# Light convolution and a routed mixture of experts in one kernel: fewer single blocks, more pairs, and later convolutions in the opening

## The chip, the cores and the metric

The kernel runs on one core of a Trainium2 chip. The metric is the device time of one execution in microseconds (us), as the median of the runs listed. The profiled execution is a run of its own; its page gives the span from its first to its last instruction.

An engine works through its own instructions in the order of the program: PE (matmul, with PEld for its weight loads), DVE (vector), ACT (activation), POOL (here the scatters) and SP (which issues the loads). One engine waits for another, or for a transfer, by semaphores.

## The reference

28,672 tokens (8 batches of 3,584) of 192 channels. First a causal convolution over 7 tokens, with the same normalised taps for the 24 channels of a head. Then each token goes to one of 8 experts, which is two dense layers of 192 to 1,024 to 192, with a gate.

```
w   = softmax over the taps of weight[h, :]                    # 8 heads, 7 taps
y   = sum over k of w[h, k] * x_padded[s + k]                  # lightweight convolution
logits = y @ w_gate ; local = sigmoid(y @ w_local)
e[s] = argmax(logits[s])  if s == 0 or local[s] < 0.5  else e[s-1]
out[s] = softmax(logits[s])[e] * (relu(y[s] @ w1[e]) @ w2[e])
```

All is float32. The expert of a token can be that of the token before it, so the choice is a scan over the sequence.

## The kernel before, in words

**Parts and units.** The tokens come in 16 parts of 1,792, numbered 0 to 15. For each part the kernel computes the convolution, the logits and the choice, and then a place for every token in a list in HBM named `slots`, in which each expert has its own region. A *unit* is 128 rows of one expert's region. Rows reach `slots` by scatters: `put()` issues one indirect DMA from POOL for 128 tokens (L844), 14 for a part, 16 for parts 0 and 1. The list `to_put` holds the scatters that have not been issued, in the order of the parts.

**Blocks.** The second half of the work is a list of *blocks* in program order, each 1, 2 or 4 units of one expert: a *single*, a *pair* or a *quad*. A block loads its expert's weights (1.5 MB, `wb`, `load_w`, L988) and its rows (`load_rows`), computes `hidden` (matmuls L1075) and `output` (L1097), scales by the gate, and scatters its rows to the result (`deliver`, L1125). The list is: 28 singles (parts 0 to 2), 43 pairs (the first of part 3), 19 quads of parts 9 to 14, then from the last part 4 quads, 4 pairs and 15 singles. Block numbers below count along this list from 0. `TURNED` is the number of opening singles, `FIRST` the number of singles and pairs before the quads. The quads go through `seven`, a scheme with seven products in place of eight (L1244), and `output_late` (L1294); the last pairs and singles through `hidden_late` (L1189) and `output_late`.

**Rows of singles and of pairs.** A single's rows come in one DMA (L996, 97.5 KB); PE transposes them (`turn`, L402) and ACT copies the result. A pair's rows come in four DMAs of 96 KB in pieces of 96 channels (L1004) and one for the heads (L1009); DVE transposes them (`turn_pair`, L1056). Both are loaded up to three blocks ahead (`ensure`, `AHEAD`). SP issues the row loads of a block, then the weights of the block three ahead. SP works in order, so a row load that waits for the part's scatters holds up what is behind it.

**When a part is ready.** `ensure(i)` looks at the blocks i to i + 3. If the part of block j is not routed, or has scatters left in `to_put`, it returns as long as j > i + 2; at j = i + 2 it finishes the route and issues the scatters that are left at once ("forced").

**The side work.** Convolution and choice of later parts run on DVE and ACT beside the blocks. They are Python generators that give a cost for each DVE instruction (0.68 for one of the convolution's, L440, of which a part has 36). At fixed places of each block `step(time)` takes instructions worth `time`: 2.1 and 1.3 in a single, 4.2, 1.2 and 3.4 in a pair. A route that is under way comes first, then the convolution. `start_conv` begins the next convolution when there is none; inside it, at the second of six channel groups (`b == 1`), the tokens of the next part are loaded (`load_x`, L150, 1.9 MB). The route begins with 96 small matmuls on PE (`logits`, L630) and ends with the places (`posi`, L810), after which the part's 14 scatters are in `to_put`, and with `tables`, which tell which expert each block has.

**Where the scatters are issued.** In a single: one in `hidden` and one in `output`. In a pair: three in `output`. The dictionary `spots` names the matmul behind which each is issued, and how many must be left over. The scatters of part 0 and the opening's route are written out by hand at the end (`puts_behind`: so many scatters behind an instruction of the route of part 1).

Of the kernel before, what the change touches and what calls it, by code (L numbers as in the profile page):

```python
# [24 lines left out]
NT = 14  # L25
PT = P * NT
NPART = N // PT
# [16 lines left out]
CAP = CAPU * UT  # L44
NU = (N + E * (UT - 1)) // UT
DUMMY = E * CAPU
EARLY = 3
SINGLES = 28
SPARE = 2


# [12 lines left out]
LAST = NPART - 1  # L64
PADS = NPART
NARROW = 8
PAIRED = 43
LEFT4 = E * (QT // 2 + UT // 8)
LEFTM = E * (QT // 2 + UT // 2)
LEFT2 = E * (BT // 2 + UT // 8)  # L70
# [41 lines left out]
def kernel(  # L112
# [35 lines left out]
    def load_x(g):  # L148
        x_sb = xs.tile([P, NX, D], F32, name="x_sb").rearrange("p t d -> p (t d)")
        nc.sync.dma_start(out=x_sb, in_=x[g])  # L150
        return x_sb.rearrange("p (b s) -> p b s", b=DQ)
# [75 lines left out]
    got, mark = {}, {}  # L227
# [125 lines left out]
    over = cst.tile([Q, Q], F32, name="over")  # L353
# [60 lines left out]
    def conv(g, x_sb):  # L414
        z = (z_tile() if g % 2 else
             ys[2].tile([P, NB, DG], F32, name="y_sb").rearrange("p b d -> p (b d)"))
        z = z[:, :NT * D].rearrange("p (b s) -> p b s", b=DQ)
        got[g] = z

        def chans(b, k):  # L420
            return x_sb[:, b, k * Q:(k + NT) * Q]

        at = {"b": 0, "first": 0}

        def firsts(more):
            while at["first"] <= min(at["b"] + more, DQ - 1):
                b = at["first"]
                nc.scalar.activation(z[:, b, :], chans(b, 0), Act.Copy, scale=c[:, b, 0:1])  # L428
                at["first"] += 1

        st["firsts"] = firsts
        firsts(0)
        yield 0
        for b in range(DQ):
            at["b"] = b
            firsts(0 if 0 < st["block"] < TURNED else 1)
            if b == 1 and 2 < g < NPART - 1:
                x_in[g + 1] = load_x(g + 1)
            for k in range(1, KC):
                nc.vector.scalar_tensor_tensor(z[:, b, :], chans(b, k), c[:, b, k:k + 1],  # L440
                                               z[:, b, :], Alu.mult, Alu.add)
                yield 0.68
# [175 lines left out]
    def logits(g, z):  # L618

        yield "pe"  # L620
        if late_p:
            both = st["bank"].tile([P, 2, 512], F32, name="ps")
            lps = [both[:, half, :TQ * Q] for half in range(2)]
        else:
            lps = [hps_p.tile([P, TQ * Q], F32, name="hps") for half in range(2)]
        begin = [min(TQ * j, NT - TQ) for j in range(4)]
        for b in range(DQ):
            for j in range(4):
                for half, rows in halves():
                    nc.tensor.matmul(lps[half][Q * j:Q * j + Q, :], lhsT=wgq[rows, b, :],  # L630
                                     rhs=z[rows, b, begin[j] * Q:(begin[j] + TQ) * Q],
                                     start=(b == 0), stop=(b == DQ - 1))
        ls = sm.tile([P, 2, TQ * Q], F32, name="ls", bufs=1)
        for half in range(2):
            nc.scalar.copy(ls[:, half, :], lps[half])
        y_sb = row_tile(g)[:, :NT, :]
        zt = z.rearrange("p b (t s) -> p t b s", s=Q)
        for t in range(0, NT, TQ):
            u = min(t + TQ, NT)
            nc.vector.transpose(y_sb[:, t:u, Y0:Y0 + D].rearrange("p t (b s) -> p t b s", s=Q),  # L640
                                zt[:, t:u])
            yield 0.24 * (u - t)
        st["turned"] = g
        lq = sm.tile([P, 2 * TQ, Q], F32, name="lq", bufs=1)
        nc.vector.transpose(lq.rearrange("p t e -> p (t e)"), ls.rearrange("p h x -> p (h x)"))
        yield 0.4
        lt = sm.tile([P, NT, E + 1], F32, name="lt")
        aside = g > EARLY + 2 and (st["cgen"] is not None or not late_p)
        if aside and late_p:
            yield "hop"  # L650
        for r in range(4):
            for j in range(4):
                t, u = TQ * j, min(TQ * (j + 1), NT)
                at = r // 2 * TQ + t - begin[j]
                e0 = r % 2 * (E + 1)
                dst = lt[Q * r:Q * r + Q, t:u, :]
                src = lq[Q * j:Q * j + Q, at:at + u - t, e0:e0 + E + 1]
                if aside:
                    nc.scalar.copy(dst, src)
                else:  # L660
                    nc.vector.tensor_copy(dst, src)
                    yield 0.12
            if aside:
                yield "hop"
        return y_sb, lt
# [166 lines left out]
    to_put = []  # L832
# [130 lines left out]
    FIRST = len(blocks)  # L963
# [2 lines left out]
    blocks += [(4, 2, i, LAST) for i in range(PAIRS)]  # L966
    blocks += [(5, 1, i, PADS) for i in range(REST)]

    AHEAD = 3
    TURNED = ONE[-1]  # L970
    SLOTS = 5
# [7 lines left out]
    def load_w(i):  # L979
# [5 lines left out]

        step = WA + WB if i > AHEAD else (WA + WB) // 3
        for x0 in range(0, WA + WB, step):
# [99 lines left out]
    def output(n, wb, xg, hT, w2):  # L1087

        yps = [yps_p.tile([P, 512], F32, name="yps") for half in range(2)]
        away = st["due"] and not (to_put and to_put[0][0] == EARLY)  # L1090
        spots = {1: {(0, 0, 1): 0} if st["block"] and not away else {},
                 2: {(0, 0, 0): 0, (0, 1, 1): 2, (2, 0, 7): 0}}[n]
        for m4 in ([0, 1, 4, 5], [2, 3, 6, 7]):
            for k in range(n):
                for m in m4:
                    for half, rows in halves():
                        ins = nc.tensor.matmul(yps[half][:, k * D:(k + 1) * D],  # L1097
                                               lhsT=hT[rows, m, k * P:(k + 1) * P],
                                               rhs=wb[rows, w2 + m * D:w2 + (m + 1) * D],
                                               start=(m == 0 and k == 0), stop=(m == FK - 1),  # L1100
                                               skip_group_check=True)
                    if len(to_put) > spots.get((m4[0], k, m), len(to_put)):
                        put(ins)
        o_sb = op.tile([P, KT, D], F32, name="o_sb")
        y = [[yps[half][:, k * D:(k + 1) * D] for half in range(2)] for k in range(n)]
        for k in range(n):
            nc.scalar.activation(o_sb[:, k, :], y[k][0], Act.Copy, scale=xg[:, k, 0:1])  # L1107

        step(1.2 if n > 1 or st["block"] > 1 else 0)
        for k in range(n):  # L1110
            nc.vector.scalar_tensor_tensor(o_sb[:, k, :], y[k][1], xg[:, k, 0:1], o_sb[:, k, :],  # L1111
                                           Alu.mult, Alu.add)

            st["hot"] = n == 1 and st["due"]
            if k == 0 and not st["hot"]:
                deliver(o_sb[:, 0, :], xg, 0)
            else:
                held.append(lambda ins, k=k: deliver(o_sb[:, k, :], xg, k, ins))
# [163 lines left out]
    def output_late(n, wb, xg, hT, rows_next=None, between=None):  # L1282

        for part, h in enumerate(hT):
# [34 lines left out]
    late_p = []  # L1319
    LATE = 3  # L1320
    SIDE = (2.4, 4.5, 2.0, 1.8)
    st = {"block": 0, "conv": 1, "cgen": None, "route": 1, "rgen": None, "routed": 1,
          "due": False, "hot": False, "since": 0, "bank": None, "over": 0, "turned": 1}

    def start_conv():
        g = st["conv"] + 1

        if (st["cgen"] is None and g < NPART and g <= st["turned"] + 2
                and (g != 3 or g in x_in and st["block"] > LATE + 2)):
            st["conv"] = g  # L1330
            st["cgen"] = conv(g, x_in.pop(g))
            next(st["cgen"])
# [48 lines left out]
    hot = hotp.tile([P, 2, NB, UT], F32, name="hot")  # L1381
# [23 lines left out]
    def puts_behind(ins, n):  # L1405
        for _ in range(n):
            put(ins)
# [7 lines left out]
    def ensure(i):  # L1415

        for j in range(len(xgs) + i, min(i + AHEAD + 1, len(blocks))):
            if j >= FIRST and j > i + 2:
                return
            g = blocks[j][3]  # L1420
            while st["routed"] < g or any(p[0] <= g for p in to_put):
                if j > (i + 2 if j < FIRST else i + 1):
                    return
                if st["routed"] < g:
                    step(4.2, late_p[0] if late_p else None, force=True)
                put()
            xgs[j] = load_rows(j)
# [10 lines left out]
    loaded = [0]  # L1438
    weights(AHEAD - 1)

# [1 line left out]
    picks = [yps_p.tile([P, 512], F32, name="yps")]  # L1442
    gather(0, ya, picks[0], range(4))
    rest(wide1)
    puts_behind(mark["lt", 1], 3)
    route1 = wide_route(1, yb, got.pop(1))
    some(route1, 2)
    taps_begun()
# [5 lines left out]
    picks.append(yps_p.tile([P, 512], F32, name="yps"))  # L1454
    gather(1, ya, picks[1], range(9))
    next(route1)
    puts_behind(mark["nf", 1], 2)
    step(1.8)
    xT, _ = turn(blocks[0][1], xgs[0])
    gather(1, ya, picks[1], range(9, NB))  # L1460
# [2 lines left out]
    step(2.4)  # L1463
    xgs[1] = gathered(picks[1])
    next(route1)
    puts_behind(mark["upto", 1], 4)
    next(route1)
    for i, (_, n, _, _) in enumerate(blocks):
        st["block"] = i
# [184 lines left out]
```

## Time and profile before

| | |
|---|---|
| time, median of 3 runs | 1298.71 us (1297.5 to 1300.3) |
| the profiled execution: time, span | 1300.09 us, 1298.3 us |
| granted TensorE clock | 0.999 |
| PE busy, PE weight loads busy | 1263.3 us (97%), 1206.5 us (93%) |
| DVE, ACT, POOL busy | 952.3 us (73%), 545.5 us (42%), 558.1 us (43%) |
| DMA | 299.59 MB, 231 GB/s over the span |
| weight loads | 109 of 1,536 KB and 12 of 512 KB |

The page names for each group of instructions the line of the kernel, the engine, the tiles, the count, busy time and idle time ahead of it, and who ended that idle time. A query of the trace gives the busy time of each engine in a stretch that one names, or the instructions of an engine in the order of time. A matmul's own duration overlaps its neighbours', so the length of a block is read from the start of its first matmul to the start of the next block's.

### The profile page before, as it was taken

The numbers are of one execution on the slowest core, as the hardware profiler recorded it, in microseconds if no ns is written. First come the engines' busy times: TensorE is split into PE (matmuls) and PEld (weight loads), VectorE is DVE, ScalarE is ACT, GpSimd is POOL, SyncE is SP. The second block draws the span as 40 slices with busy tenths as digits, with TensorE's granted clock in tenths as the row PEclk, the third lists the DMA queues.
The fourth block names the chain that finished last, engine by engine and source line by source line (L and its number), as shares of the span: only waits on it lengthen the run. The fifth ranks groups of instructions, "written<-read, shape, count | busy, mean of one in ns | idle before, by whom it ended". The sixth has DMA issues, their size and how long they took to land. (4 is left out here: it accounts for less than half of the span.)

```text
span 1298.3 us, 39551 instructions
## 1 busy us (share of the span) xinstructions
PE 1263.3 (97%) x15406; PEld 1206.5 (93%) x15406; DVE 952.3 (73%) x2504; ACT 545.5 (42%) x1208; POOL 558.1 (43%) x619
## 2 busy tenths in 40 slices
PE   9899989999999999999999999999999999999997
PEld 7789988998999999999999998999999999999997
DVE  5979878999898989999897999985885444431111
ACT  5345554334243442434425444543444444432332
POOL 4544354444344444444445455345466533421211
PEclk9999999999999999999999999999999999999999
DMA  5799997999787887978888546464655635536894
GB/s 196 262 364 390 340 359 238 341 322 321 225 288 266 248 289 228 292 260 252 288 228 243 157 122 178 105 180 123 167 158 156 183 103 158 155 97 194 276 323 156
DMA packets 182674, 299.59 MB, mean 231 GB/s; under 512 B 145872, under 2 KB 157191, under 8 KB 166738
## 3 DMA queue, kind: packets, MB, share of 16 engines
q1 hardware_dynamic: 160160, 251.79, 61.4%
q0 software_dynamic: 22320, 45.22, 10.7%
q8 instruction: 123, 2.02, 0.7%
q14 instruction: 69, 0.57, 0.1%
q10 hardware_dynamic: 2, 0.00, 0.0%
HBM read 251.35 MB, written 46.07 MB: 229 GB/s over the span
## 5 line engine op out<-in xcount | busy, mean ns | idle before, releaser
L1125 POOL DMA_INDIRECT out_dram<-o_sb,head x201 | 209.0, 1040 | 445.7 <-DVE o_sb L1309 269.1
L1075 PE MATMUL hps<-xT,wb 64*128 64x256 f32 (+1 forms) x3408 | 317.7, 337 | 4.7 <-issue 3.2
L1097 PE MATMUL yps<-wb,hT 64*128 64x192 f32 x3648 | 316.1, 324 | 3.7 <-DVE o_sb L1111 2.7
L1097 PEld LDWEIGHTS yps<-wb,hT 64*128 64x128 f32 x3648 | 301.6, 187 | 8.9 <-DVE o_sb L1111 3.9
L1075 PEld LDWEIGHTS hps<-xT,wb 64*128 64x128 f32 x3408 | 281.1, 187 | 30.7 <-issue 8.0
L1294 PE MATMUL ps<-wb,hot 64*128 64x192 f32 x3680 | 308.0, 323 | 0.9 <-issue 0.4
L844 POOL DMA_INDIRECT slots<-y_sb,posi x228 | 232.6, 1020 | 170.3 <-PE yps L1097 75.8
L1294 PEld LDWEIGHTS ps<-wb,hot 64*128 64x128 f32 x3680 | 299.3, 187 | 4.9 <-issue 2.5
L1084 ACT ACTIVATE hT<-hps 128x512 f32<-128x512 f32 (+1 forms) x284 | 130.4, 510 | 160.1 <-PE hps L1075 128.3
L440 DVE SCALAR_TENSOR_TENSOR y_sb<-x_sb,c,y_sb 128x448 f32<-128x448 f32 x252 | 172.7, 695 | 21.9 <-ACT y_sb L428 15.8
L440 DVE SCALAR_TENSOR_TENSOR z<-x_sb,c,z 128x448 f32<-128x448 f32 x252 | 172.8, 695 | 20.8 <-ACT z L428 11.6
L1309 DVE SCALAR_TENSOR_TENSOR o_sb<-ps,head,o_sb 128x192 f32<-128x192 f32 x115 | 43.2, 411 | 136.5 <-ACT o_sb L1304 130.3
L1304 ACT ACTIVATE o_sb<-ps,head 128x192 f32<-128x192 f32 x115 | 43.0, 418 | 204.2 <-PE ps L1294 198.3
L1107 ACT ACTIVATE o_sb<-yps,head 128x192 f32<-128x192 f32 x86 | 31.5, 417 | 155.6 <-PE yps L1097 79.8
L1168 DVE STREAM_TRANSPOSE xT<-y_sb 128x768 f32<-128x768 f32 (+1 forms) x65 | 54.8, 871 | 54.6 <-PE ps L1189 33.0
L1244 PE MATMUL ps<-xT,wb 64*128 64x256 f32 x736 | 88.6, 376 | 1.1 <-DVE xT L1220 1.1
L1244 PEld LDWEIGHTS ps<-xT,wb 64*128 64x128 f32 x736 | 77.7, 187 | 2.1 <-issue 1.5
L1189 PE MATMUL ps<-xT,wb 64*128 64x128 f32 (+1 forms) x912 | 64.3, 294 | 0.1
L1265 DVE TENSOR_TENSOR hot<-xps,hot 128x512 f32<-128x512 f32 x46 | 31.5, 685 | 44.7 <-PE xps L1244 44.6
L1125 POOL DMA_INDIRECT out_dram<-o_sb,xg x28 | 30.1, 1076 | 78.0 <-DVE o_sb L1111 52.0
L1189 PEld LDWEIGHTS ps<-xT,wb 64*128 64x128 f32 x912 | 62.7, 188 | 0.4 <-DVE xT L1168 0.4
L1266 ACT ACTIVATE hot<-hot 128x512 f32<-128x512 f32 x46 | 29.0, 630 | 64.9 <-DVE hot L1265 55.7
(296 smaller groups left out, 1399.8 us busy)
## 6 DMA issues: line engine op xcount, KB each, us to landing
wb<-in_w_dram SPq DMA_DIRECT2D x109, 1536.0 KB
x_sb<-in_x_dram SPq DMA_DIRECT2D x14, 1920.0 KB
y_sb<-slots SPq DMA_DIRECT2D x92, 192.0 KB
hot<-slots SPq DMA_DIRECT2D x172, 96.0 KB
wb<-in_w_dram SPq DMA_DIRECT2D x12, 512.0 KB
slots<-y_sb,posi POOLq DMA_INDIRECT x228
out_dram<-o_sb,head POOLq DMA_INDIRECT x201
x_sb<-in_xb_dram SPq DMA_DIRECT2D x4, 768.0 KB
```

The lines of the kernel that those rows point to most:

```text
L440: nc.vector.scalar_tensor_tensor(z[:, b, :], chans(b, k), c[:, b, k:k + 1], z[:, b, :], Alu.mult, Alu.add)
L844: ins = nc.gpsimd.indirect_dma_start(out=slots[:, :], in_=rows, in_offset=None, out_offset=bass.IndirectOffsetOnAxis(ap=to, axis=0)).ins
L1075: ins = nc.tensor.matmul(hps[half][:, j, w], lhsT=wb[rows, w1 + f0:w1 + f0 + P], rhs=xT[rows, d, w], start=(d == 0 and j == 0), stop=(d == ...
L1084: nc.scalar.activation(hT[:, m:m + 2, w], hps[half][:, :, w], Act.Relu)
L1097: ins = nc.tensor.matmul(yps[half][:, k * D:(k + 1) * D], lhsT=hT[rows, m, k * P:(k + 1) * P], rhs=wb[rows, w2 + m * D:w2 + (m + 1) * D], ...
L1125: sent = nc.gpsimd.indirect_dma_start(out=out, in_=o, in_offset=None, out_offset=bass.IndirectOffsetOnAxis(ap=xg.bitcast(I32)[:, k, 1:2], ...
L1168: nc.vector.transpose(xT.rearrange("p d (j t) -> p j d t", t=Q)[:, js], rows[:, js].rearrange("p j (d t) -> p j d t", t=Q))
L1189: nc.tensor.matmul(hps[:, half, j, :], lhsT=wb[rows, f0:f0 + P], rhs=xT[rows, d, :], start=(d == 0 and j == 0), stop=(d == KD - 1), skip_g ...
L1244: ins = nc.tensor.matmul(to[:, half, j, :], lhsT=b[rows, j * P:(j + 1) * P], rhs=a[rows, :], start=(first and j == 0), stop=True, skip_gro ...
L1294: ins = nc.tensor.matmul(yps[:, half, k * D:(k + 1) * D], lhsT=h[two][rows, side, j, k * P:(k + 1) * P], rhs=wb[rows, f * D:(f + 1) * D], ...
L1304: nc.scalar.activation(o_sb[:, k, :], yps[:, 0, k * D:(k + 1) * D], Act.Copy, scale=xg[:, at + k, 0:1])
L1309: nc.vector.scalar_tensor_tensor(o_sb[:, k, :], yps[:, 1, k * D:(k + 1) * D], xg[:, at + k, 0:1], o_sb[:, k, :], Alu.mult, Alu.add)
```

## The change

Three things change in the plan and four in the order of the work.

- `EARLY` 3 to 2, `SINGLES` 28 to 21, `PAIRED` 43 to 46. By the plan's arithmetic the list becomes 21 singles (parts 0 and 1), 46 pairs (3 of part 2, then 7 a part for parts 3 to 8, one of part 9), the same 19 quads, 4 quads, 5 pairs and 14 singles. The number of units computed stays 229; the blocks are 109 in place of 113.
- In the convolutions of parts 3 and 4 the tokens of the next part are loaded at `b == 3` in place of `b == 1`.
- A convolution of part 4 or later begins only when the block number is more than two past the block in which its tokens were loaded; this ends with the quads.
- The scatters of part 3 ("the fourth part") get more places: two more in `output` of a single or a pair, which makes three in a single and five in a pair.
- `ensure` finishes a part two blocks ahead only if no more than 3 of its scatters are left; else one block ahead. For single blocks nothing changes.
- In the opening, of the scatters of part 0 one more is issued behind `lt` and one more behind `nf`, and two fewer behind `upto`.
- `ASIDE = 5` keeps the old value of `EARLY + 2`, and the test against `EARLY` in `output` becomes a test against 3, as it was.

```diff
-EARLY = 3
-SINGLES = 28
+EARLY = 2
+SINGLES = 21
...
-PAIRED = 43
+PAIRED = 46
...
-            if b == 1 and 2 < g < NPART - 1:
+            if b == {3: 3, 4: 3}.get(g, 1) and 2 < g < NPART - 1:
                 x_in[g + 1] = load_x(g + 1)
+                st["loaded"] = st["block"]
...
-        aside = g > EARLY + 2 and (st["cgen"] is not None or not late_p)
+        aside = g > ASIDE and (st["cgen"] is not None or not late_p)
...
-        away = st["due"] and not (to_put and to_put[0][0] == EARLY)
+        away = st["due"] and not (to_put and to_put[0][0] == 3)
         spots = {1: {(0, 0, 1): 0} if st["block"] and not away else {},
                  2: {(0, 0, 0): 0, (0, 1, 1): 2, (2, 0, 7): 0}}[n]
+        if to_put and to_put[0][0] == 3:
+            spots.update({1: {(2, 0, 3): 0}, 2: {(2, 0, 2): 0, (2, 1, 6): 0}}[n])
...
         if (st["cgen"] is None and g < NPART and g <= st["turned"] + 2
+                and (late_p or g < 4 or st["block"] > st["loaded"] + 2)
                 and (g != 3 or g in x_in and st["block"] > LATE + 2)):
...
             while st["routed"] < g or any(p[0] <= g for p in to_put):
-                if j > (i + 2 if j < FIRST else i + 1):
+                wait = sum(p[0] <= g for p in to_put) if st["routed"] >= g else NT
+                if j > (i + 2 if j < TURNED or j < FIRST and wait <= 3 else i + 1):
                     return
...
-    puts_behind(mark["lt", 1], 3)
+    puts_behind(mark["lt", 1], 4)
...
-    puts_behind(mark["nf", 1], 2)
+    puts_behind(mark["nf", 1], 3)
...
-    puts_behind(mark["upto", 1], 4)
+    puts_behind(mark["upto", 1], 2)
```

3 lines of the change are left out of this document (2 added, 1 removed).

## The prediction

> **What bounds the kernel now.** I read the page first (busy shares and slices), then the busy time by stretches, then PE, SP, POOL and DVE in the order of time around the blocks that change. PE is busy almost everywhere, so a change is worth what it does to the length of the blocks on PE, and what makes PE wait.
>
> ```profile
> span 1298.3 us, 39551 instructions
> ...
> PE 1263.3 (97%) x15406; PEld 1206.5 (93%) x15406; DVE 952.3 (73%) x2504; ACT 545.5 (42%) x1208; POOL 558.1 (43%) x619
> ...
> DVE  5979878999898989999897999985885444431111
> ...
> DMA  5799997999787887978888546464655635536894
> ```
>
> The reader sees that from slice 2 to slice 20 (65 to 680 us) DVE runs near 90% too, and DMA at 70% and more: the opening singles and the pairs. Next the stretches, cut at the first matmul of a block. Columns: length, busy time of PE, PEld, DVE, ACT, POOL with instruction counts, clock, DMA share, GB/s.
>
> ```profile
> 162.16:167.60 5.44, 5.44 (x87) 5.44 (x86) 4.94 (x19) 2.89 (x9) 3.09 (x3) 1.00 0.85 286
> 173.04:182.09 9.05, 6.16 (x89) 5.78 (x87) 8.22 (x13) 3.70 (x11) 4.50 (x5) 1.00 0.84 293
> 182.09:227.35 45.26, 42.75 (x683) 40.23 (x680) 35.11 (x123) 21.07 (x66) 21.09 (x21) 1.00 0.79 288
> 260.63:271.01 10.38, 10.38 (x116) 9.85 (x115) 9.60 (x44) 3.09 (x7) 3.05 (x4) 1.00 1.00 307
> 227.35:305.52 78.17, 77.39 (x977) 71.92 (x977) 74.24 (x182) 26.93 (x56) 32.72 (x33) 1.00 1.00 327
> ...
> 695.53:863.40 167.87, 163.65 (x1828) 156.89 (x1826) 151.54 (x338) 80.79 (x137) 80.80 (x84) 1.00 0.54 145
> 1008.66:1168.23 159.57, 159.57 (x1732) 157.55 (x1731) 68.46 (x114) 68.65 (x96) 58.89 (x65) 1.00 0.51 140
> 1178.61:1188.99 10.38, 10.38 (x116) 10.38 (x115) 1.72 (x3) 2.90 (x6) 1.95 (x2) 1.00 0.59 191
> 1215.45:1220.73 5.28, 5.28 (x84) 5.28 (x83) 0.99 (x2) 1.74 (x5) 0.97 (x1) 1.00 0.78 234
> ```
>
> In this order: single 18 undisturbed, block 20 (the last single before part 2), the seven singles of part 2 (21 to 27), a pair undisturbed, the first seven pairs, the first eight quads, eight quads without side work, a pair and a single of the end. A pair costs PE 10.38 where two opening singles cost at least 10.88; and the seven singles took 45.26 where seven undisturbed ones take 38.08.
>
> **1. Seven singles become three pairs.** The seven singles hold one route's 96 small matmuls, and so will the three pairs (part 4's). What these cost between two pairs is seen here:
>
> ```profile
> 227.35 5.45 PE L1075 MATMUL hps<-xT,wb 64*128 64x256 f32 x48 [0.52 <-issue]
> 232.64 5.37 PE L1097 MATMUL yps<-wb,hT 64*128 64x192 f32 x64
> 237.84 5.35 PE L1075 MATMUL hps<-xT,wb 64*128 64x256 f32 x48
> 243.02 5.37 PE L1097 MATMUL yps<-wb,hT 64*128 64x192 f32 x64
> 248.32 1.90 PE L630 MATMUL hps<-z,wg 64*32 64x128 f32 x96
> 250.14 1.14 PE L1075 MATMUL hps<-xT,wb 64*128 64x256 f32 x8
> ```
>
> Block 29 goes from 237.84 to 250.14, 12.30, so the route adds 1.92. Three pairs: 3 x 10.38 + 1.92 = 33.06, against 45.26: **-12.2**. Do pairs stall as these singles did (5.3 beyond 38.08 + 1.92)? The first seven pairs took 78.17; less 72.66 for seven undisturbed, that is 5.51 for two routes, 2.76 each, and nothing else. So the bound on the dear side is 0.8 more, -11.4. DVE's transposition of a pair's rows (0.98, row below) replaces PE's; in 78.17 us DVE was busy 74.24 with it, so it is covered. Each pair also loads weights once for two units; four weight loads go in all.
>
> **2. One unit more at the end.** 229 units stay. The front's singles and pairs take 21 + 92 = 113 in place of 28 + 86 = 114, so the end has 14 singles and 5 pairs for 15 and 4: 10.38 - 5.28 = **+5.1**. Nothing waits there: PE is busy for all of both rows.
>
> **3. The wait in block 20.** Block 20 took 9.05 where 5.44 is undisturbed, 3.61 lost. PE, then POOL, then SP:
>
> ```profile
> 167.60 2.88 PE L1075 MATMUL hps<-xT,wb 64*128 64x128 f32 x48
> ...
> 173.04 3.50 PE L1075 MATMUL hps<-xT,wb 64*128 64x128 f32 x48
> 179.29 0.34 PE L402 MATMUL xps<-ident,xg 64*128 64x64 f32 x4 [2.74 <-DMA xg<-slots]
> ...
> 166.20 1.15 POOL L844 DMA_INDIRECT slots<-y_sb,posi  x1 [0.71 <-PE yps L1097]
> ...
> 163.75 0.33 SPq L988 DMA_DIRECT2D wb<-in_w_dram  x1
> 164.14 1.30 SPq L150 DMA_DIRECT2D x_sb<-in_x_dram  x1
> 175.01 1.25 SPq L996 DMA_DIRECT2D xg<-slots  x2
> ```
>
> Part 2's last scatter ended on POOL at 167.35, but SP could issue the rows only at 175.01, 7.66 later: weights and part 5's tokens had gone out just ahead. The change moves these tokens twelve convolution instructions on, into block 20 and on SP behind the rows and weights of block 23. How a pair's rows then come is bounded by part 3's in the run before, where only weights (issued at 210.99) were ahead:
>
> ```profile
> 214.97 0.96 POOL L844 DMA_INDIRECT slots<-y_sb,posi  x1 [0.30 <-issue]
> ...
> 210.99 0.33 SPq L988 DMA_DIRECT2D wb<-in_w_dram  x1
> 220.38 2.37 SPq L1004 DMA_DIRECT2D hot<-slots  x4
> 222.80 0.40 SPq L1009 DMA_DIRECT2D head<-slots  x1
> ...
> 226.32 0.98 DVE L1056 STREAM_TRANSPOSE xT<-hot 128x768 f32<-128x768 f32 x1 [1.31 <-DMA hot<-slots]
> ```
>
> Scatter's end to first row load 4.45, from there to the transposition 5.94, itself 0.98. For block 21: 167.35 + 4.45 + 5.94 + 0.98 = 178.7, and block 20 undisturbed ends at 178.5. So 0.2 is lost in place of 3.61: **-3.4**. The other bound: the 7.66 stays, then 181.9 against 182.09, -0.2. I take the first, as the weights alone were ahead in its row too.
>
> **4. Part 3 at block 24.** It is wanted sooner: 182.09 - 3.4 + 33.06 = 211.8, where block 28 had it at 227.35. Its places are there in good time:
>
> ```profile
> 160.89 0.17 DVE L810 CAST posi<-pos 128x14 int32<-128x14 f32 x1
> ...
> 172.07 0.99 POOL L844 DMA_INDIRECT slots<-y_sb,posi  x1 [0.30 <-issue]
> ```
>
> Its first scatter went at 172.07, behind part 2's, its last (above) ended at 215.93. With the new places blocks 19 and 20 issue three each, block 21 five, and the last three are forced when block 22 begins, at about 189.1. A scatter takes 0.96 and 0.30 to the next; with a delivery among them the last ends by 194.5. With the slow 7.66: 194.5 + 7.66 + 5.94 + 0.98 = 209.1, 2.7 before it is wanted; with 4.45, 5.9. So nothing is lost; without that cover each us late is a us of PE. On POOL five scatters and two deliveries are 7 x 1.3 = 9.1 of a pair's 10.38; the deliveries behind them wait, and two result buffers of two units each give them a block's time. On SP the row loads of 24 and 25 hold up the weights of block 25, wanted only at 222. Cost 0.
>
> **5. Later loads, the three blocks.** A convolution is 36 x 0.68 = 24.5 of step time, of which a single gives 3.4 and a pair 8.8. That of part 4 begins one block later (block 14) and by these costs still ends in block 21; that of part 5 begins in block 23, and the steps of 21 and 22 go partly unused. DVE gains nothing from having more to do there, and part 4 is wanted at block 31 only. What is late next is the quads. Each hold pushes the later parts back, and by the step costs part 13's logits come in the second quad, where they came just before the last pair:
>
> ```profile
> L630 PE MATMUL hps<-z,wg x576: 266/269/295, 136.4 to 684.8; 64*32 64x128 f32 x192
> ```
>
> (684.8 is the last in the opening's PSUM tiles.) Counted in steps, 13 quads in place of 11 have full side work. The first eight quads took 167.87 - 159.57 = 8.3 longer than eight without side work, less 1.92 for a route 6.4, 0.8 a quad: **+1.6**. Bounds: 0, and 4 if five quads stall.
>
> **6. The opening's scatters.**
>
> ```profile
> 51.68 0.94 POOL L844 DMA_INDIRECT slots<-y_sb,posi  x1 [0.30 <-issue]
> 52.92 0.94 POOL L844 DMA_INDIRECT slots<-y_sb,posi  x1 [0.30 <-issue]
> ```
>
> Two of the last four move ahead, so the last ends two issues of 1.24 sooner, 2.5. The rows that wait for them are block 2's, and PE has two blocks without them; I take 0, with -2.5 as the bound.
>
> **Sum.** -12.2 + 5.1 - 3.4 + 1.6 = -8.9. The profiled execution: span 1298.3 to 1289.4 (its time, 1300.09, is 1.8 above its span). Against the median of the runs shown, 1298.71, which is 1.4 under the profiled run: 1289.8.
>
> **Rivals.**
>
> *The wait in block 20 stays.* For it: the pair's rows take five DMAs in place of one, and the weights of 163.75 are still ahead of the scatter. Against it: 4.45 in the row above. It takes back 3.2: 1293.0. [...]
>
> *The first pairs are bound by DMA.* For it: the DMA share of a pair is 1.00, that of single 18 0.85, and blocks 21 to 24 have part 5's tokens and the faster scatters on top. While only rows were read, DMA moved little:
>
> ```profile
> 220.40:224.30 3.90, 3.90 (x65) 3.90 (x63) 2.92 (x12) 1.09 (x4) 1.41 (x3) 1.00 0.66 155
> ```
>
> 155 GB/s against 307. Against it: at a share of 1.00 the first seven pairs lost nothing that isn't their routes'. If blocks 21 to 27 each lost 1 us: 1296.8. [...]
>
> *Part 3 misses block 24* (the other side). If more than 3 scatters are left when block 22 begins, `ensure` returns and they are forced at block 23 (199.5). With 8 left the last ends at about 209.7; + 7.66 + 5.94 + 0.98 = 224.3, 12.5 late: 1302.3. It decides from a last scatter that ends after 206, where the loss passes 8.9. Against it: by the counts only three are left.
>
> *More is gained*: the 2.5 of the opening reaches PE, and the quads cost nothing more: 1285.7.
>
> **How the numbers follow.** Forecast 0.55, by itself 1287.5 to 1292; the wait stays 0.19; DMA-bound 0.07; part 3 misses 0.06; more gained 0.13. 0.2% is 2.6 us, about what a measurement of this kernel can tell from no change. Under 1296.1 lie the forecast, the wait, the greater gain and a small part of the DMA case: 0.88; within, most of the DMA case: 0.06; slower, part 3: 0.06. Low 1285.7, down to the greater gain; high 1295.5, past the wait and short of the two dear cases.
>
> **What would show it.** Block 21 starts by 178.5 to 179 and its rows load at about 172 (3); the pairs from 21 are 10.4 each, with one route 12.3 (1); block 24 starts at about 212 and its DVE transposition waits for no DMA (4); three sets of logits lie in the quads, and the first quad begins 15.6 sooner than 695.53 (5); 5 pairs and 14 singles at the end (2). Wrong would be a wait of PE at block 21 or 24 for `hot`, row loads of block 24 after 205, or pairs of 11 and more between 178 and 290.

## The result, and the profile after

The changed kernel took 1309.52 us (median of 19 runs, 1304.99 to 1314.6), the kernel before 1300.53 us beside it (19 runs, 1296.27 to 1306.67). The ratio is 1.0067, with a 95% interval of 1.0051 to 1.0083: slower by 0.7%, where 0.7% faster had been forecast. The profiled execution took 1311.33 us, with a span of 1309.6 us and a granted clock of 0.991 (0.999 before). The page's rows that answer to those of before:

```profile
span 1309.6 us, 39043 instructions
...
PE 1268.4 (97%) x15186; PEld 1209.1 (92%) x15186; DVE 955.6 (73%) x2507; ACT 535.6 (41%) x1164; POOL 557.4 (43%) x619
...
DVE  5879886998989989999898988984887435421111
...
DMA  5799988968787888978897636455564645546794
```

PE has 220 matmuls less than before and is busy 5 us longer, where the clock is lower: the 115 or 116 matmuls of a pair are busy 10.38 at a clock of 1.00 (block 21) and 13.02 at 0.88 (block 30). Where, the stretches tell. Busy time by stretches of the changed kernel (length, busy time of PE, PEld, DVE, ACT, POOL with counts, clock, DMA share, GB/s), cut as before: block 20, blocks 21 and 22, the three new pairs together, blocks 30 and 36, the 43 pairs from block 24, all quads.

```profile
175.56:184.23 8.67, 7.01 (x85) 5.89 (x83) 5.98 (x10) 2.62 (x7) 5.96 (x7) 1.00 0.78 180
184.23:194.61 10.38, 10.38 (x115) 9.85 (x115) 10.06 (x16) 2.60 (x5) 5.12 (x5) 1.00 1.02 386
194.61:214.25 19.64, 16.48 (x210) 14.06 (x210) 7.94 (x24) 3.89 (x9) 6.76 (x7) 0.83 0.73 250
184.23:224.63 40.40, 37.24 (x434) 33.67 (x434) 26.94 (x77) 10.12 (x22) 13.99 (x14) 0.92 0.86 303
289.34:304.09 14.75, 13.02 (x116) 11.65 (x114) 13.47 (x42) 4.01 (x8) 6.89 (x7) 0.88 0.94 307
357.99:372.50 14.51, 12.90 (x115) 11.55 (x114) 11.82 (x39) 2.90 (x6) 8.10 (x8) 0.88 0.58 185
224.63:696.27 471.64, 467.29 (x5587) 438.20 (x5587) 430.02 (x1186) 183.17 (x446) 209.79 (x205) 0.99 0.83 263
696.27:1174.46 478.19, 468.72 (x5260) 453.35 (x5259) 329.49 (x739) 212.65 (x329) 225.25 (x241) 1.00 0.54 150
```

Block 21 is the 10.38 of the forecast. Block 22, a pair with one route (12.3 forecast), took 19.64 at a clock of 0.83; blocks 30 and 36, plain pairs, 14.75 and 14.5 at 0.88. These three are 16 us longer than such blocks undisturbed, where forecast and result lie 20 us apart. The instructions of block 22 in order of time, PE, then ACT, then POOL:

```profile
194.61 5.35 PE L1077 MATMUL hps<-xT,wb 64*128 64x256 f32 x48
202.84 3.56 PE L631 MATMUL hps<-y_sb,wg 64*32 64x128 f32 x70 [2.89 <-ACT hT L1086]
...
202.19 1.08 ACT L1086 ACTIVATE hT<-hps 128x512 f32<-128x512 f32 x2 [5.96 <-remote]
...
194.88 0.96 POOL L845 DMA_INDIRECT slots<-y_sb,posi  x1 [0.74 <-PE yps L1101]
196.14 0.96 POOL L845 DMA_INDIRECT slots<-y_sb,posi  x1 [0.30 <-issue]
197.41 0.98 POOL L1129 DMA_INDIRECT out_dram<-o_sb,head  x1 [0.30 <-issue]
198.69 0.96 POOL L845 DMA_INDIRECT slots<-y_sb,posi  x1 [0.30 <-issue]
199.96 0.96 POOL L845 DMA_INDIRECT slots<-y_sb,posi  x1 [0.30 <-issue]
201.23 0.96 POOL L845 DMA_INDIRECT slots<-y_sb,posi  x1 [0.30 <-issue]
```

The first half of `hidden`'s 48 matmuls had ended by 197.4, but the trace records the semaphore updates that they raise only at 202.11 and 202.15, almost five microseconds late, and ACT read the result from 202.19. In those microseconds POOL issued six indirect transfers back to back, 0.30 apart, and the last ended at 202.19. Block 30, PE and POOL:

```profile
294.52 2.27 PE L1101 MATMUL yps<-wb,hT 64*128 64x192 f32 x25
297.73 0.32 PE L1101 MATMUL yps<-wb,hT 64*128 64x192 f32 x1 [0.93 <-issue]
298.45 0.32 PE L1101 MATMUL yps<-wb,hT 64*128 64x192 f32 x1 [0.40 <-issue]
299.17 5.09 PE L1101 MATMUL yps<-wb,hT 64*128 64x192 f32 x37 [0.40 <-issue]
...
291.96 0.96 POOL L845 DMA_INDIRECT slots<-y_sb,posi  x1 [7.40 <-issue]
...
297.07 0.98 POOL L1129 DMA_INDIRECT out_dram<-o_sb,head  x1 [0.30 <-issue]
```

Five transfers from 291.96 to 298.05, again without a pause; PE waits for nothing that the profile shows ("issue"), goes on at 299.17 and then has the half clock (0.50) from 299.6 to 303.0. Block 36 is the same with five from 360.33 to 366.41. In its first trace the kernel before has no run of five after its opening.

**Two kinds of chip.** The later runs, each set on one chip beside the kernel before, met a difference without which no number below can be read. The last column counts, in the profiled trace of the kernel named, the matmuls that raise a semaphore and have no recorded update of it within 1 us of their end: it came later, or its record is missing.

| set, chip | kernel before, median | changed kernel, ratio (95%) | matmuls without a prompt update |
|---|---|---|---|
| the first comparison | 1300.5 | 1.0067 (1.0051 to 1.0083) | 115 of 1,099 (changed), 140 of 1,132 (before) |
| chip 12 | 1280.7 | not run | 0 (`loads_back`) |
| chip 2, first set | 1280.5 | 0.9951 (0.9932 to 0.9971) | 0 (changed), 0 (before) |
| chip 10 | 1280.3 | 0.9968 (0.9958 to 0.9979) | 0 (changed) |
| chip 6 | 1300.4 | not run | 138 of 1,080 (`runs_many`) |
| chip 2, second set | 1281.2 | 0.9970 (0.9954 to 0.9985) | 0 (changed) |
| chip 0 | 1296.0 | not run | 125 of 1,099 (`spread22_b`) |

The column mixes the two: in the changed kernel's first trace 1,028 updates are recorded for 1,099 such matmuls, on chip 2 1,101. Certainly late are those that come more than 1 us after every matmul that can have raised them: 57 and 51 in the first comparison (changed, before), none on chip 2, the last 15 us of the program aside.

I call them *late* chips (6, 0, and by its trace the first) and *prompt* chips (12, 2, 10). These are names: only chip 2 was measured twice, so it is not shown that the difference belongs to the chip and not to the occasion. Undisturbed pairs and end singles take 10.38 and 5.28 on both. On the prompt chips the change gains 0.3 to 0.5%; on the late one it loses 0.7%.

### The profile page after: what moved, and what is told of

It reads as the page before. It is cut to its first block, busy times and chain, and to the rows that moved or that the text cites. A ratio compares the mean times of both kernels' runs of the same rounds, so it can differ in the third digit from the quotient of the medians.

```text
span 1309.6 us, 39043 instructions
## 1 busy us (share of the span) xinstructions
PE 1268.4 (97%) x15186; PEld 1209.1 (92%) x15186; DVE 955.6 (73%) x2507; ACT 535.6 (41%) x1164; POOL 557.4 (43%) x619
## 4 chain that ended last, share of the span: by engine, by line
PE 91%; DVE 4%; issue 2%; DMA 1%; ACT 0%; another core or an unknown queue 0%; POOL 0%; SPq 0%; POOLq 0%; DVEq 0%; ACTq 0%
PE yps L1101 23%; PE hps L1077 22%; PE ps L1298 22%; PE ps L1248 12%; PE ps L1193 5%; PE xps L1248 3%; PE hps L631 2%; DMA y_sb<-slots 1%; PE yps L610 1%; PE hps L252 1%; DVE y_sb L441 1%; PE ps L631 0%; PE hps L189 0%; DVE o_sb L1313 0%
## 5 line engine op out<-in xcount | busy, mean ns | idle before, releaser
L1129 POOL DMA_INDIRECT out_dram<-o_sb,head x208 | 215.4, 1036 | 453.6 <-DVE o_sb L1313 267.5
L1077 PE MATMUL hps<-xT,wb 64*128 64x256 f32 (+1 forms) x3216 | 311.8, 344 | 3.8 <-issue 3.7
L1077 PEld LDWEIGHTS hps<-xT,wb 64*128 64x128 f32 x3216 | 274.8, 187 | 29.4 <-issue 7.0
L1086 ACT ACTIVATE hT<-hps 128x512 f32<-128x512 f32 (+1 forms) x268 | 127.5, 527 | 172.4 <-PE hps L1077 120.4
L1248 PE MATMUL ps<-xg 64*128 64x256 f32 x368 | 49.2, 380 | 5.7 <-POOL xg L1214 3.2
```

Source lines behind the costliest of these rows:

```text
L1077: ins = nc.tensor.matmul(hps[half][:, j, w], lhsT=wb[rows, w1 + f0:w1 + f0 + P], rhs=xT[rows, d, w], start=(d == 0 and j == 0), stop=(d == ...
L1086: nc.scalar.activation(hT[:, m:m + 2, w], hps[half][:, :, w], Act.Relu)
L1129: sent = nc.gpsimd.indirect_dma_start(out=out, in_=o, in_offset=None, out_offset=bass.IndirectOffsetOnAxis(ap=xg.bitcast(I32)[:, k, 1:2], ...
L1248: ins = nc.tensor.matmul(to[:, half, j, :], lhsT=b[rows, j * P:(j + 1) * P], rhs=a[rows, :], start=(first and j == 0), stop=True, skip_gro ...
```

## The experiments

Theory A: while POOL issues indirect transfers back to back, PE's semaphore updates are held; up to three are hidden, five or more stop PE, and the clock then halves. Its rival B: each stop has a cause of its own (the logits that stand in block 22, PE's instruction fetches at 30 and 36). That it is PE that fetches there is a guess: the trace has 3 packets of instructions from 290 to 300 (queue q14) and does not say for which engine.

**`pause`** (chip 12). In `deliver`, blocks 20 to the last pair:

```
+        if 20 <= st["block"] < FIRST:
+            for _ in range(5):
+                nc.gpsimd.memset(quiet, 0.0)      # 128 x 192
```

> The changed kernel with five small memsets on GpSimd (192 columns each, about 1.3 us together) ahead of each delivery from block 20 to the last pair, so that no more than three or four indirect transfers follow one another on GpSimd. Theory A (GpSimd run): while GpSimd issues indirect transfers back to back, TensorE's semaphore updates are held; a run of three is hidden, one of five or six stops PE and the clock then halves. Then blocks 22, 30 and 36, which took 19.64, 14.75 and 14.52 us, take about 12.3, 10.4 and 10.4, no half clock stands between 60 and 1300 us, and the time is 1311.3 - 7.3 - 4.4 - 4.1 = about 1295.5 (1293 to 1299). Theory B (block 22 is stopped by the logits that the three-block hold puts into it, 30 and 36 by PE's own instruction fetches beside busy DMA): the three blocks stay as long, time 1307 to 1313.

1278.72 us, ratio 0.9989 (0.9974 to 1.0003). Blocks 22, 30 and 36 took 12.77, 11.19 and 10.38. But the kernel before took 1280.7 here, and the next run, on the same chip, shows the stops gone without pauses. That run was also 4 us shorter, with 462.9 in the 43 pairs where `pause` took 464.5: memsets ahead of every delivery seem to cost something (five take 1.53 us in `runs_many`, where 1.3 was expected).

**`opening_back`** (chip 12): `puts_behind` 3, 2, 2, 4 again in place of 4, 3, 2, 2.

> The changed kernel with the opening's scatters as before (3, 2, 2, 4 in place of 4, 3, 2, 2). Theory A: the first run on GpSimd has eight transfers and not nine and ends about 1.3 us sooner; PE's gaps at 42 us and the half clock from 47.0 to 50.4 go, the last four make a run of four in block 0; block 1 begins 1 to 2 us sooner than 56.80, the time falls by as much to 1307 to 1309. Theory B (the opening waits for its tokens alone): block 1 at 56.8, time as the changed kernel's.

1274.77 us, ratio 0.9959 (0.9946 to 0.9971). Runs of eight and nine transfers stand in the trace, and blocks 22, 30 and 36 took 12.56, 11.02 and 10.38. So A as first put is wrong: a run alone stops nothing. On prompt chips the opening's edit moves no time that can be told: block 21 began at 172.7 here and at 172.9 in `pause`.

**`loads_back`** (chip 12): `if b == 1` again, and `start_conv` without `st["block"] > st["loaded"] + 2`.

> The changed kernel with parts 5's and 6's tokens loaded at the second convolution column again and without the three-block hold. Theory A: the route's steps fall into other blocks, so the runs of five at blocks 30 and 36 go or move, and the time follows the number of runs of five or more (about 5 us each with the half clock); block 20 waits for rows again (9.0). One set of logits fewer lies in the quads, which get 2 to 4 us shorter. Between 1298 and 1308. Theory B: block 22 takes about 12.3 without the hold (7.3 less), 30 and 36 stay: about 1300.

1275.77 us, ratio 0.9971 (0.9953 to 0.9989). Block 20 took 7.07 (5.72 with the later loads), the 43 pairs 460.4 (462.6 to 463.4 with the hold and without pauses). The quads still hold three sets of logits and take 468.4.

**`before_runs`** (chip 12), the kernel before with, at one matmul of a pair's `output`, `for _ in range(many): put(ins)` in place of the spread scatters, `many` 3, 4, 5, 6, 8 for parts 5 to 9, and 24 memsets for parts 10 and 11.

> The kernel before with runs made on purpose: in one pair for each of the parts 5 to 9, three, four, five, six and eight scatters are put behind one matmul in place of three spread ones, and for parts 10 and 11 one pair has 24 small memsets on GpSimd (about 6 us, no transfer) in the same place. Theory A: the pairs with three take 10.4, with four 10.4 to 11.5, with five about 14.5, with six 15 to 17, with eight 17 to 20; the half clock follows where PE stood; memsets cost nothing if it is the transfers, as much if it is a busy GpSimd. Time about 1315 to 1325. Theory B: every one of them 10.4, time 1300.

1281.17 us beside 1280.66. All of these pairs took 10.4 to 10.5, with a route 12.0 to 12.3. So on this chip runs cost nothing, made by hand or not.

**`after_again`, `before_again`** (chip 2), the two kernels themselves.

> The changed kernel itself, once more. In the first four runs the kernel before took 1280.7 us where it had taken 1300.5 beside the first run of the changed kernel, and runs of eight or nine transfers on GpSimd stopped nothing there, so the time and the stops seem to belong to a chip. Theory A1 (the stops at blocks 22, 30 and 36 come only where the trace also shows TensorE's semaphore updates late, on a slower chip): beside a kernel before of about 1300 the three blocks stop again and the ratio is about 1.005 to 1.008; beside one of about 1280 they take 12.3 to 12.8, 10.4 to 11.2 and 10.4, and the ratio is 0.994 to 0.999. Theory C (the first profile was a chance): the ratio is below 1 on either.

> The kernel before itself, for its trace on the same chip. A1: on a chip with about 1280 us its seven singles take about 41.5 us (45.26 in the first trace), block 20 about 7.3 (9.05), the first block starts at about 45; on one with about 1300 us as in the first trace.

1273.83 us, ratio 0.9951 (0.9932 to 0.9971), as A1 has it. The profiled executions took 1274.14 and 1280.02. Stretches of the kernel before (block 20; the seven singles; all quads), then of the changed one (block 20; block 22; blocks 21 to 23; 43 pairs; quads):

```profile
168.85:176.15 7.30, 5.96 (x90) 5.80 (x89) 7.05 (x12) 3.47 (x11) 4.57 (x5) 1.00 0.74 225
176.15:218.22 42.07, 41.41 (x683) 39.61 (x680) 36.31 (x126) 21.63 (x67) 20.74 (x22) 1.00 0.87 327
682.00:1148.40 466.40, 463.49 (x5165) 453.67 (x5163) 320.48 (x724) 210.18 (x320) 221.99 (x237) 1.00 0.54 149
```

```profile
167.72:173.44 5.72, 5.55 (x84) 5.36 (x83) 5.58 (x10) 2.30 (x7) 4.43 (x5) 1.00 0.81 193
183.82:196.31 12.49, 12.49 (x212) 11.88 (x212) 8.46 (x25) 3.89 (x9) 7.07 (x8) 1.00 1.00 369
173.44:206.69 33.25, 33.25 (x437) 32.12 (x436) 26.56 (x74) 10.12 (x22) 16.09 (x16) 1.00 0.86 294
206.69:669.30 462.61, 461.67 (x5589) 436.20 (x5588) 431.21 (x1191) 183.36 (x446) 209.55 (x205) 1.00 0.86 275
669.30:1137.50 468.20, 465.55 (x5259) 454.08 (x5259) 330.68 (x738) 212.64 (x329) 225.49 (x241) 1.00 0.55 154
```

The same program as on the late chip, and its block 22 is all PE, 12.49 of 12.49, at full clock, though POOL issued nine transfers in a row from 181.3 to 193.0.

**`pause_runs`** (chip 2), the changed kernel with `pause`'s memsets in blocks 20 to 39 and runs of 4, 5, 6 and 8 scatters for parts 8 to 11, made as in `before_runs`.

> The changed kernel with five small memsets on GpSimd ahead of each delivery of blocks 20 to 39, and runs of four, five, six and eight scatters behind one matmul in a pair of parts 8, 9, 10 and 11. Theory A1 on a slow chip: blocks 22, 30 and 36 take 12.3, 10.4 and 10.4, and the pairs with five, six and eight scatters in a row take 14.5, 15 to 17 and 17 to 20, with four 10.4 to 11.5; on a fast chip all pairs 10.4 and about 1278 us. Theory B (logits and fetches): 19.6, 14.7 and 14.5 stay on a slow chip and the runs cost nothing.

1277.47 us. The blocks with six and with eight, each with a route:

```profile
552.90:565.23 12.33, 12.33 (x210) 11.27 (x208) 10.95 (x24) 5.23 (x12) 7.81 (x8) 1.00 0.76 229
606.85:619.26 12.41, 12.41 (x214) 11.25 (x210) 9.10 (x23) 4.72 (x10) 8.00 (x8) 1.00 0.77 230
```

PE is busy for all of both. On a prompt chip runs cost nothing.

**`both_back`** (chip 2): `opening_back` and `loads_back` together.

> The changed kernel with the opening's scatters and the loads as before and without the hold: of the change, the plan (21 singles, 46 pairs) and part 3's scatters remain. If each of these edits cost what it seemed to on the fast chip (ratios 0.9959 and 0.9971 without them), this one has 0.993 to 0.996 there, the best of all; if the two edits pull against each other (the load in front of part 2's last scatters, block 20 at 7.1 in place of 5.7) it stays at 0.997. On a slow chip 0.995 to 1.003, by the runs of five that are left.

1274.84 us, ratio 0.9962 (0.9947 to 0.9976), within the interval of the changed kernel's. So plan and part 3's places carry the gain.

**`after_third`, `spots_back`, `hold_back`, `before_late`** (chip 10). `spots_back` drops the two lines `if to_put and to_put[0][0] == 3: spots.update(...)`; `hold_back` drops `and (late_p or g < 4 or st["block"] > st["loaded"] + 2)`; `before_late` is the kernel before with `b == {3: 3, 4: 3}.get(g, 1)`.

> The changed kernel a third time. Theory D (the steps of the change hold, and the first comparison was taken in a condition that slows both kernels by 20 us and more and stops PE at blocks 22, 30 and 36): beside a kernel before of about 1280 us the ratio is 0.993 to 0.997 as in the run before; beside one of about 1300 us it is above 1.004 again and the three stops are there. Theory C (a matter of the chip alone, each with its own ratio): anything between.

> The changed kernel without part 3's added places for scatters. Theory D: more than three scatters are left when block 22 begins, they are forced a block later, and block 24 waits for its rows, 5 to 12 us: 1279 to 1286 beside a kernel before of 1280. Rival (the forced scatters of block 22 alone bring part 3 in time): as the changed kernel, 1274.

> The changed kernel without the three-block hold, the later loads kept. Theory D: the third set of logits in the quads comes from the shorter front (four blocks fewer), not from the hold, so it stays in the first quad and the quads take 468 us as with the hold; block 20 stays at 5.7; time within 1.5 us of the changed kernel's. Rival (the prediction's step 5: the hold pushes part 13 into the quads): two sets of logits in the quads and 1.6 us less.

> The kernel before with the later loads alone (parts 4's and 5's tokens at the fourth convolution column). Theory D: block 20 no longer waits 1.3 us for its rows (7.29 to about 5.8), nothing else moves, 1.3 us less: ratio 0.999. Rival (the prediction's rival, the wait stays): block 20 as before, ratio 1.

`after_third`: 0.9968 (0.9958 to 0.9979), as D has it. `spots_back`: 1.0016 (1.0006 to 1.0026); what block 24 waited for, on PE and on DVE:

```profile
211.00 3.33 PE L1077 MATMUL hps<-xT,wb 64*128 64x256 f32 x16 [4.73 <-issue]
...
209.93 0.98 DVE L1058 STREAM_TRANSPOSE xT<-hot 128x768 f32<-128x768 f32 x1 [8.50 <-DMA hot<-slots]
```

Part 3 misses block 24, as the prediction's rival on the other side describes: 4.9 us there, 3 more in the pairs behind. `hold_back`: 0.9951 (0.9935 to 0.9968). Its 43 pairs and its quads, then those of `after_third`:

```profile
206.95:667.78 460.83, 460.81 (x5588) 434.15 (x5586) 427.82 (x1185) 182.33 (x445) 207.15 (x205) 1.00 0.87 276
667.78:1135.88 468.10, 465.39 (x5259) 453.88 (x5258) 330.85 (x738) 212.63 (x329) 225.59 (x241) 1.00 0.55 154
```

```profile
205.86:668.83 462.97, 461.95 (x5587) 435.92 (x5586) 431.55 (x1193) 183.33 (x446) 209.33 (x205) 1.00 0.87 274
668.83:1137.04 468.21, 465.50 (x5261) 453.97 (x5259) 330.67 (x738) 212.62 (x329) 225.53 (x241) 1.00 0.56 154
```

The hold costs 2.1 us in the pairs and nothing in the quads, which have three sets of logits with and without it. `before_late`: 0.9994 (0.9985 to 1.0004); block 20 took 5.72 in place of 7.30, the wait for rows gone, as D has it, but the seven singles behind took 43.1, a microsecond more, and the gain in time can't be told from none.

**`runs_many`, `hold_opening_back`** (chip 6, late). What was still open: whether the runs cause the stops where updates are late. `runs_many` is the changed kernel with, each in one pair, six scatters in a row, six with five memsets after each second, 24 memsets, and eight in a row. `hold_opening_back` is `hold_back` with `opening_back`.

> The changed kernel with, each in one pair, six scatters in a row (part 8), six with five small memsets after each second one (part 9), 24 small memsets and no transfer (part 10) and eight scatters in a row (part 11). If this run falls into the condition of the first comparison (kernel before about 1300 us): theory A (runs of transfers on GpSimd stop PE there) has 15 to 17 us for the pair of part 8, 10.4 for 9 and 10, 17 to 20 for 11, and the stops at blocks 22, 30 and 36; theory D' (the condition slows everything and the runs are only its sign) 10.4 to 12 for all four. In the condition of the runs since (about 1280): all four 10.4, about 1275 us.

> The changed kernel without the three-block hold and with the opening's scatters as before. The hold cost about 2 us in the pairs of the run before (463.0 against 460.8), the opening's edit moved the time by nothing that could be told: 1272 to 1274 beside a kernel before of 1280, ratio 0.993 to 0.996. If the opening's edit gains after all (its wait for block 2's rows, 2.6 us, in block 1): 1274 to 1276.

`runs_many` took 1323.81 us (one run) beside 1300.43. The pair with six (and a route), the pair with most of the six with pauses (and a route) and the one behind it, the one behind the memsets, the one with eight; and from POOL's instructions the memsets:

```profile
465.51:484.13 18.62, 15.36 (x211) 12.67 (x210) 10.08 (x25) 4.63 (x10) 9.01 (x10) 0.91 0.59 182
536.13:549.77 13.64, 12.89 (x212) 11.40 (x210) 11.98 (x19) 5.31 (x14) 10.73 (x19) 1.00 0.92 328
549.77:561.00 11.23, 11.14 (x116) 9.82 (x115) 9.04 (x15) 7.26 (x21) 6.05 (x6) 1.00 0.76 239
593.76:604.24 10.48, 10.48 (x116) 9.95 (x114) 10.27 (x17) 4.32 (x12) 6.51 (x11) 1.00 0.97 369
658.58:674.86 16.28, 12.83 (x115) 10.27 (x115) 9.56 (x16) 6.59 (x20) 8.40 (x9) 1.00 0.48 165
```

```profile
587.95 7.51 POOL L1120 MEMSET quiet<- 128x192 f32 x24 [0.76 <-PE yps L1108]
```

Six in a row cost 6.6 us (18.62 against 12.0), eight 5.9; six with pauses 2.5 in all, where A had nothing; 7.5 us of GpSimd work without transfers nothing, neither in that block (12.0, with a route) nor in the next. The six follow two deliveries without a pause, so both are runs of eight transfers, and that they cost about the same is no measure of six against eight; the eight cost less than A's 17 to 20 us for the pair. The natural stops came again: 18.58, 13.20 and 14.60 in blocks 22, 30 and 36. `hold_opening_back` took 1301.83 us, ratio 1.0003 (0.9984 to 1.0022): without the hold, and with the opening as before, the two runs of five do not form, and blocks 30 and 36 take 10.38 and 12.01 (with a route); block 22 keeps its run of six and its 19.6. No late chip had a run that takes back the hold alone.

**`spread22`, `after_fifth`** (chip 2), **`spread22_b`** (chip 0, late). On top of `hold_opening_back`:

```
+        if st["block"] == TURNED and k == 0:      # deliver of block 21
+            pause()                               # five memsets
...
+                if i == TURNED + 1 and to_put and i not in paused:   # ensure, block 22
+                    paused.add(i); pause()
                 put()
```

> The changed kernel without the hold and with the opening's scatters as before, and with five small memsets (1.5 us) on GpSimd ahead of block 21's first delivery and ahead of the three forced scatters of block 22, so that the run of six becomes two, one and three. Theory A: where the kernel before takes about 1300 us, block 22 takes 12.3 to 14 in place of 19.69, and if part 3's rows come 0 to 2 us late at block 24 for it, the time falls by 5 to 7 us, ratio 0.995 to 0.998 (1.0003 without the memsets); where it takes about 1280, nothing stopped there, ratio 0.995 to 0.997. Theory D' (the stop of block 22 has to do with its logits, the run is a sign of it): 19 to 20 us stay, ratio 1.000.

> The changed kernel beside it: ratio 1.005 to 1.008 and stops at blocks 22, 30 and 36 where the kernel before takes about 1300 us, 0.995 to 0.997 and no stops where it takes about 1280.

> The same kernel as spread22 once more, for the condition in which the kernel before takes about 1300 us. Theory A: there block 22 takes 12.3 to 14 in place of 19.69 and the ratio is 0.995 to 0.998; theory D': 19 to 20 and 1.000. Where the kernel before takes about 1280, 0.995 again.

On chip 2: 0.9952 (0.9939 to 0.9966), the changed kernel 0.9970 (0.9954 to 0.9985). On the late chip 0: 1288.2 us, ratio 0.9946 (0.9931 to 0.9961). Block 22 of `hold_opening_back`, then of `spread22_b`, both late:

```profile
192.10:211.70 19.60, 16.78 (x210) 14.04 (x208) 11.23 (x29) 4.63 (x10) 6.99 (x7) 0.83 0.70 236
```

```profile
189.35:201.84 12.49, 12.48 (x212) 11.21 (x209) 9.74 (x20) 4.45 (x10) 9.41 (x17) 1.00 0.99 349
```

Ten memsets on an engine that has time go with 7.1 us less in block 22. The two traces are of two late chips, 6 and 0, and `hold_opening_back` wasn't run on chip 0. But in the five late traces (these two, `runs_many` and the first two) every run of five transfers or more behind the opening lies at a pair that stops, 18.6 to 19.7 us with a route and 13.2 to 16.3 without one, and no other pair up to the quads takes more than 13.8 and 11.3. And `runs_many` stopped two pairs by runs that were put in, one of them without logits. So A holds on late chips as far as it says that such runs stop PE, while B and D' (the logits in block 22, or the slower condition itself, do it and the run is only a sign) fall. How a run comes to hold PE's updates is not shown. This version beats the kernel before on both kinds of chip; the changed kernel does so on one.

## Why the prediction was wrong, point by point

Spans by stage, in us, from the rows above and those of before (the last column is the pair of executions on chip 2):

| step | forecast | first comparison | prompt chip |
|---|---|---|---|
| start of block 21 (3, 6) | -3.4 | 182.09 to 184.23, +2.1 | 176.15 to 173.44, -2.7 |
| seven singles to three pairs (1, 4) | -12.2 | 45.26 to 40.40, -4.9 | 42.07 to 33.25, -8.8 |
| 43 pairs and the quads (5) | +1.6 | +3.5 and +5.5 | -1.2 and +1.8 |
| the end (2) | +5.1 | 130.1 to 135.1, +5.1 | 129.8 to 134.9, +5.1 |
| sum | -8.9 | +11.3 | -5.8 |

**The step that failed is 4**, in one sentence of it: "On POOL five scatters and two deliveries are 7 x 1.3 = 9.1 of a pair's 10.38", with cost 0 behind it. POOL had the time, and part 3 was there for block 24. What was not priced is that transfers so close become a run without a pause, six in block 22, and on that chip such a run stops PE: 7.3 us in block 22. No row of the trace before had one outside the opening, and the text gave that unseen thing no bounds.

That is the largest piece of the 20.2 us between the two sums, not all of it. 5.5 lie ahead of block 21 (steps 3 and 6). 3.5 lie in the 43 pairs, where the stops at blocks 30 and 36 cost 8.5 and the other pairs give 5.0 back, and 3.9 in the quads beyond the 1.6 forecast (step 5).

**Step 5** had nearly the right amount for the quads on the prompt chip (+1.8) for the wrong reason, which is luck. The third set of logits lies in the quads of every version with the new plan, with the hold or without; `before_late`, with the old plan, has two. The hold's real price on a prompt chip is 2.1 us in the pairs. On the late one the runs of five at blocks 30 and 36, 4.4 and 4.1 us, seem to be its price too, as they are gone in `hold_opening_back`. The quads' +5.5 there isn't settled: against the 472.7 before, `hold_opening_back` took 480.6 and `spread22_b` 473.8, on other late chips, and no experiment was made on them.

**Step 3** was right that the load was in the way: moved alone, the load takes block 20 from 7.30 to 5.72 (5.64 forecast). Its size came from the late chip, whose block 20 lost 3.6, while a prompt one loses 1.9. On the late chip the wait for rows went as well, but block 20 still took 8.67, with PE's gaps put down to "issue" and to ACT, beside POOL's transfers. The rival that the wait in block 20 stays does not agree with `before_late`, whose block 20 took 5.72. Whether the order of issue on SP or the load's own transfer held the rows back, no run tells.

**Step 1**: three pairs take 33.25 where 33.06 was forecast; the singles that they replace took 42.07 on the prompt chip and not 45.26, so less was to be had. **Step 2** came out to the tenth. **Step 6**, 0, holds on prompt chips, but by luck, as the reason given (PE has two blocks without these rows) is not what happened. Block 1 of the kernel before, on chip 2, waited for block 2's rows; in the changed kernel that wait is short, and block 3 pays:

```profile
58.09 0.34 PE L402 MATMUL xps<-ident,xg 64*128 64x64 f32 x4 [2.63 <-DMA xg<-slots]
```

```profile
54.90 0.34 PE L402 MATMUL xps<-ident,xg 64*128 64x64 f32 x4 [0.45 <-DMA xg<-slots]
...
70.01 2.70 PE L1101 MATMUL yps<-wb,hT 64*128 64x192 f32 x29 [2.25 <-DVE o_sb L1115]
```

On late chips the ninth transfer of the opening's run seems to cost, and step 6 had neither that nor a bound for it: block 0 began at 50.3 and 48.6 with the edit, at 45.9, 45.6 and 45.0 without, and block 3 at 68.9 and 67.1 against 66.4, 65.6 and 65.0. No run on a late chip takes back this edit alone.

**The rivals.** DMA-bound first pairs fell: block 21 took 10.38 at a DMA share of 1.02. Part 3 missing block 24 is real, but only without the added places. The rival that happened was not among them.

## What to carry to other kernels

Count the indirect transfers that GpSimd issues without a pause, not only its busy time, and keep them below five where updates come late: in the five late traces every run of five or more behind the opening lay at a pair that stopped, while with no more than four in a row (`spread22_b`, 196.89 to 201.68) block 22 took 12.49. On a prompt chip eight in a row cost nothing (12.41, `pause_runs`). A run can form where POOL has just stood idle, 7.4 us ahead of those at blocks 30 and 36; that those behind a waiting scatter pile up there is a reading of the rows, not a test. Ten memsets at one place cost nothing that could be told (0.9952 on a prompt chip beside 0.9970 for the changed kernel); five ahead of every delivery seemed to cost some. And price a step from more than one chip where one can: two terms here (45.26 and 9.05) were losses of one kind of chip, and the kernel's verdict changed sign with the chip.

## What the runs showed of the hardware that was not expected

The kernel before has two times, 1280 and 1296 to 1300 us, with every undisturbed block as long (pairs 10.38, end singles 5.28): on three chips PE's semaphores are raised promptly, and in the other traces more than a tenth of the raising matmuls have no update recorded within 1 us. What makes a chip late stays open. The record has a span and a granted clock for every run, figures of the profiler, and none that is known to be without it; so whether the lateness, and with it the loss of 0.7%, is there when nothing is traced is not known. The late traces hold 15,000 semaphore events where the prompt ones of the same program hold 21,400; that something was amiss with the records there is plain from it, and no run shows what.

After each of the three stops in the changed kernel's first trace the clock stood at half: for 6.8 us in block 22 (204.0 to 210.8, granted 0.50), for 3.4 at block 30 (299.6 to 303.0) and for 3.4 at block 36 (367.8 to 371.3). At block 30 the recorded gaps ahead of the half clock are 0.93, 0.40 and 0.40 us. What sets the length of these stretches, and how long a gap brings one on, is not shown.
